# Two of the four down sums of the first feed-forward half: from VectorE's adds in SBUF to ScalarE copies and accumulating DMAs into DRAM

## The chip, the cores and the metric

The kernel runs on one core of a Trainium2 chip. The metric is the device time of one execution in microseconds. In profiles the engines are PE (TensorE: matmuls, with PEld for the loading of their stationary operand), DVE (VectorE), ACT (ScalarE), POOL (GpSimd) and SP (SyncE, which only issues DMAs here). An engine works through its own instructions in the order of the program. ScalarE and GpSimd can also issue DMAs, and such an issue stands in the engine's order like any other instruction: if it has to wait, everything behind it on that engine waits too.

## The reference

The kernel computes one transformer block on 2048 tokens of width 576: an attention with a compressive memory, then a SwiGLU feed-forward network. The change lies in the second. With h the normalised and modulated input, gb a gate and x the stream after the attention:

```python
def _B_ref(x, w_gate, w_up, w_down):      # w_gate, w_up: 576 x 4608, w_down: 4608 x 576
    g = _silu(x @ w_gate)
    u = x @ w_up
    return (g * u) @ w_down
...
h = _layernorm(x, axis=-1) * (1 + cb) + sb
x = x + gb * _B_ref(h, B_w_gate, B_w_up, B_w_down)
```

All inputs and outputs are fp32.

## The kernel before

The attention takes about the first third of the time. Its last step adds its result to the input and stores the stream x to DRAM (`xD`, four tensors of 512 tokens, each 128 partitions x 4 x 576). The feed-forward part then runs in two halves of 1024 tokens: t = 0 and t = 1. Each half is a loop over 18 pairs of 128-wide slices of the hidden dimension (p = 0 to 17), and each pair has 14 steps (k = 0 to 13).

*Gate and up products.* For a pair, gate (z = 0) and up (z = 1) are each computed by seven products of a Strassen-like scheme, one per step (`step`, `prod`, line 1202: seven matmuls of 512 columns). The products are gathered in three PSUM banks A, B and C. After the first product of a z, ScalarE copies bank A to a new bank B (line 1248, "B<-A"); the next product that adds to A, two steps later, has to wait for that copy. Two more copies (line 1231, "tb", "tc") play the same part later. `fin` (lines 1215 to 1226) joins banks and copies into the activations.

Every operand of a matmul is split into a rounded high part (a copy by ScalarE, lines 1166, 1191, 1266: `wh`, `dh`, `ah`) and a low rest (a subtraction by VectorE, lines 1167, 1192, 1267: `wl`, `dl`, `al`). The splits of weights are made five steps ahead of their product.

*Weights.* The gate and up weights of a pair come into two tiles `O` (z = 0 and 1). In the half t = 0 GpSimd makes the sums of weight blocks that the scheme needs (`sum_o`, line 1157), four per tile, in the steps 4 to 7 for z = 0 of the next pair and in the steps 10 and 11 for z = 1. These sums are stored to DRAM for the second half (`store_o`, line 1141, "oD<-O"), and ScalarE issues these stores: for z = 0 at step 11, for z = 1 at step 13, the last step of a pair. A tile O can be loaded again once VectorE has made the last `wl` from it. GpSimd also scales the down weights (`mul_d`, line 1180) and makes their sums (`sum_d`, line 1185), which ScalarE's queue stores at step 12 (line 1525, "wd").

*Down sums of the first half.* The down product of a pair is worked off in the steps of the next pair. `plain` handles one of its 8 chunks, in the steps 4 to 11: c runs over b (which 512 tokens), h (which 288 of the 576 output columns) and a half of the tokens. A chunk is twelve matmuls of 288 columns into two PSUM banks `pd` (two such buffers), and VectorE adds the result to an fp32 accumulator in SBUF (line 1327). There are four accumulators, `acc[2 + h + 2 * b]`; each is loaded beforehand with the matching part of `xD` (`load_res`, in steps that the table `RS` lists), so that it ends as the output. After the last pair it is stored to the output by a DMA that ScalarE issues (`store`, line 1295), three steps after its last chunk. The last pair of the first half is thus worked off in the first loop (p = 0) of the second half.

In the second half the down product is also done by a seven-product scheme (`down`, line 1306) with seven accumulators; `new_acc` makes three of them (1, 6, 7) when the pool `p6`, with the working tiles of `prep2` (the preparation of the second half's input), is closed.

The order of the work is written out by hand: the loops over p and k issue everything, and an engine gets its instructions in that order.

Of the kernel before, what the change touches and what calls it, by code (L numbers as in the profile page):

```python
# [7 lines left out]
F32 = mybir.dt.float32  # L8
# [3 lines left out]
ALU = mybir.AluOpType  # L12
# [3 lines left out]
P = 128  # L16
# [19 lines left out]
NSG = 7  # L36
CH = (1, 1, 1, 1, 2, 1, 0, 1, 1, 1, 1, 2, 1, 0)
CH0 = ((0, 0, 0, 0, 1, 1, 1, 1, 1, 1, 1, 1, 0, 0), (0, 0, 0, 1, 1, 1, 1, 1, 1, 1, 1, 0, 0, 0))
RS = {(0, 5): 2, (0, 6): 4, (0, 8): 3, (0, 10): 5, (1, 9): 2, (1, 11): 3, (1, 13): 4}
KS = (2, 3, 4, 5)  # L40
KA = ((5, 3), (6, 5), (7, 7), (3, 8))
ASRC = {5: (1, 1), 6: (0, 0), 7: (0, 1), 3: (1, 0)}
# [30 lines left out]
def block(ctx: ExitStack, tc: tile.TileContext, x, wqk, wv, wo, beta, wgu, wd, c, w_mod, out):  # L73
    nc = tc.nc
    def pool(stk, name, bufs=1, **kw):
        return stk.enter_context(tc.tile_pool(name=name, bufs=bufs, reuse_waits="tile", **kw))
# [9 lines left out]
    def run(g):  # L86
        for _ in g:
            pass
# [56 lines left out]
    xD = [dr.tile([P, 4, D], F32, tag=f"xD{s}", name=f"xD{s}") for s in range(NSEG)]  # L145
# [769 lines left out]
    NPR = NF // 2  # L915
# [362 lines left out]
    def new_acc(accp, ms):  # L1278
        for m in ms:
            acc[m] = accp.tile([P, 4, 288], F32, tag=f"acc{m}", name=f"acc{m}")  # L1280
# [3 lines left out]
    def load_res(t, m):  # L1284
        b, h = RES[m]
        nc.sync.dma_start(acc[m], xD[2 * t + b][:, :, 288 * h:288 * h + 288])
# [5 lines left out]
    def store(t, b, h, src, c=None):  # L1292
        r = 1024 * t + 512 * b
        i0, i1 = (0, 4) if c is None else (2 * c, 2 * c + 2)
        (nc.sync if t else nc.scalar).dma_start(out[r + 128 * i0:r + 128 * i1, 288 * h:288 * h + 288].rearrange("(i p) d -> p i d", p=P),
                          src[:, i0:i1])
# [16 lines left out]
    def plain(t, p, c):  # L1313
        b, h, c = c // 4, c // 2 % 2, c % 2
        pd = ps.tile([P, 2, L], F32, tag="dn", name="pd", bufs=2)
        for i in range(2):
            tk = slice(128 * (2 * c + i), 128 * (2 * c + i) + 128)
            k = 0
            for f in range(2):
                ah, al = AP[p % 2, (f, b)]  # L1320
                dh, dl = DP[p % 2, (f, h)]
                for a, w in ((ah, dh), (ah, dl), (al, dh)):
                    nc.tensor.matmul(pd[:, i, :288], lhsT=a[:, tk], rhs=w, start=(k == 0), stop=(k == 5))  # L1323
                    k += 1
        d = x11[1] if t and b and h else acc[2 + h + 2 * b]
        o = d[:, 2 * c:2 * c + 2]
        nc.vector.tensor_tensor(o, o, pd[:, :, :288], op=ALU.add)  # L1327
        if p == NPR - 1:
            if t:
                store(t, b, h, d, c)  # L1330
            elif c == 1:
                return lambda: store(t, b, h, d)

    def comb(j):
        d, b = ((2, 1), (0, 5), (6, 1), (5, 6), (3, 5), (7, 6), (4, 7), (0, 7))[j]
        d = acc[d] if d else x11[1]
        nc.vector.tensor_tensor(d, d, acc[b], op=ALU.add)

    def is_plain(t, p):
        return t == 0 or p >= NPR - 2  # L1340

    with tc.manual_schedule():
# [85 lines left out]
        p6 = ExitStack()  # L1428
# [12 lines left out]
        for t in range(2):  # L1441
            for p in range(NPR):
# [4 lines left out]
                if t == 0 and p == 1:  # L1447
                    p7.close()
                    x2p = pool(p6, "x2p")
                    g2 = prep2(x2p)  # L1450
                if t == 0 and p == NPR - 1:
                    run(g2)
                    p6.close()
                    accq = pool(p4, "acq")
                    new_acc(accq, (1, 6, 7))
# [3 lines left out]
                for k in range(14):  # L1459
# [68 lines left out]
                    if prev is not None and is_plain(*prev):  # L1528
                        if k in (0, 2):
                            ij = (1, 0) if k == 0 else (0, 1)  # L1530
                            prep_a(prev[1] % 2, ij, PA[ij])
                        if CH0[t][k]:
                            f = plain(*prev, chunk)
                            if f:
                                late[k + 3] = f
                            chunk += 1
                        due(k)
                    elif prev is not None:
                        for j in range(4):
                            if k == KS[j]:  # L1540
                                sum_a(j)
                        if k == 0:
                            prep_a(prev[1] % 2, 2, PA[1, 0])
                        for j, kk in KA:
                            if k == kk:
                                prep_a(prev[1] % 2, j, PA[ASRC[j]])
                        for _ in range(CH[k]):
                            down(*prev, chunk)
                            chunk += 1
                    if last and 1 <= k < 9:  # L1550
                        comb(k - 1)
                    if p == 0 and (t, k) in RS:
                        load_res(t, RS[t, k])
                    if is_plain(t, p):
# [20 lines left out]
        for c in range(8):  # L1575
            plain(*prev, c)
            if c == 0:
                flush()
# [52 lines left out]
```

## Time and profile before

| | |
|---|---|
| median of 3 runs | 1906.63 us |
| lowest, highest | 1906.19, 1909.42 us |
| span of the profiled execution, first to last instruction | 1906.7 us |
| TensorE busy | 1870.6 us (98%) |
| VectorE busy | 1507.7 us (79%) |
| ScalarE busy | 933.8 us (49%) |
| GpSimd busy | 579.1 us (30%) |

The profile gives the span of its execution and no other time of it. It shows one execution. A busy share is that of an engine's instructions; issues of DMAs are not counted as busy. A row of the groups names a line of the kernel, the engine, the operation, the tile written and the tiles read, the shapes and the count, then the busy time and the mean of one in ns, and after the second bar the idle time of the engine just before them with what ended it. Rows of the timeline begin with the start and the length in us and end, in brackets, with the idle time before and its releaser; ACTq and SPq are DMA issues of ScalarE and SyncE. A row of the chain of waits has start, length and what ran. A row of the waits says who waited for whom: in total, how often, and the longest.

### The profile page before, as it was taken

What the parts mean: (1) busy time and instruction counts of PE and PEld (TensorE: products, weight loads), DVE (VectorE), ACT (ScalarE), POOL (GpSimd) and SP (SyncE); (2) the same over time, 40 slices, a digit from 0 to 9 for tenths busy, and PEclk for the clock granted to TensorE, in tenths of its full rate; (3) what the DMA queues carried; (4) which work ended last, traced back from release to release, by engine and by line L of the source; (5) the groups of instructions that cost most, each with busy time, mean ns of one, the idle gap of its engine ahead of it and who ended that gap; (6) DMA issues with size and microseconds to landing.
All of it is one profiled execution on the core that took longest, in us unless ns stands there. A gap on an engine that the chain in (4) does not pass through costs nothing.

```text
span 1906.7 us, 30703 instructions
## 1 busy us (share of the span) xinstructions
PE 1870.6 (98%) x10927; PEld 1560.4 (82%) x10927; DVE 1507.7 (79%) x3277; ACT 933.8 (49%) x2060; POOL 579.1 (30%) x783
## 2 busy tenths in 40 slices
PE   7999999999999999999999999999999999999999
PEld 4878866676766788888888888888888888888888
DVE  6566358878886888888888888867888888888887
ACT  1222267768767543454454454444445454454542
POOL 5212236455556545445445435400000000000000
PEclk9999999999999999999999999999999999999999
DMA  6767555446654854554454554477333333333331
GB/s 196 253 216 251 200 191 155 131 137 172 186 159 134 301 204 148 170 190 142 170 188 139 186 162 129 152 258 237 102 124 102 98 103 101 123 102 104 104 106 61
DMA packets 179424, 304.31 MB, mean 160 GB/s; under 512 B 26152, under 2 KB 107688, under 8 KB 177352
## 3 DMA queue, kind: packets, MB, share of 16 engines
q1 hardware_dynamic: 150696, 245.29, 41.2%
q10 hardware_dynamic: 28576, 57.07, 8.4%
q8 instruction: 86, 1.41, 0.3%
q14 instruction: 66, 0.54, 0.1%
HBM read 187.98 MB, written 113.77 MB: 158 GB/s over the span
## 4 chain that ended last, share of the span: by engine, by line
PE 91%; DVE 3%; ACT 2%; DMA 2%; POOL 1%; issue 1%; SPq 0%; ACTq 0%; POOLq 0%; DVEq 0%
PE A L1202 23%; PE pd L1323 13%; PE C L1202 12%; PE pd L1306 9%; PE B L1202 6%; PE pp L99 5%; PE s L599 4%; PE av L619 4%; PE s L182 4%; PE pv L99 3%; PE pw L729 3%; PE pn L800 1%; ACT Pt L602 1%; PE px L640 1%; PE pm L448 1%
## 5 line engine op out<-in xcount | busy, mean ns | idle before, releaser
L1202 PE MATMUL A<-y,wh 128*128 128x512 f32 x1152 | 406.3, 393 | 3.1 <-ACT B L1248 2.5
L187 DVE CUSTOM_DVE_ANT_0 junk<-s,tri 128x256 bf16<-128x256 f32 (+3 forms) x512 | 228.5, 486 | 69.0 <-PE s L182 61.8
L1167 DVE TENSOR_TENSOR wl<-O,wh 128x256 fp32r<-128x256 f32 x504 | 262.1, 525 | 3.4 <-ACT wh L1166 2.9
L1202 PEld LDWEIGHTS A<-y,wh 128*128 128x128 f32 x1152 | 217.1, 188 | 47.0 <-ACT B L1248 3.2
L1202 PE MATMUL A<-y,wl 128*128 128x512 f32 x576 | 226.9, 394 | 0.0
L602 ACT ACTIVATE Pt<-s 128x512 f32<-128x512 f32 (+1 forms) x352 | 187.9, 559 | 70.9 <-PE s L599 66.6
L1157 POOL TENSOR_TENSOR O<-O 128x384 f32<-128x384 f32 x140 | 159.4, 1151 | 175.9 <-DMA O<-in_wgu_dram 73.8
L1311 DVE TENSOR_TENSOR acc<-acc,pd 128x576 f32<-128x576 f32 x216 | 162.3, 752 | 58.7 <-PE pd L1306 52.1
L1202 PE MATMUL C<-y,wh 128*128 128x512 f32 x576 | 203.3, 394 | 2.8 <-DMA y<-yD 2.4
L1166 ACT CAST wh<-O 128x256 fp32r<-128x256 f32 x504 | 196.7, 405 | 0.7 <-issue 0.7
L1323 PE MATMUL pd<-dh,al 128*128 128x288 f32 x640 | 189.0, 295 | 0.0
L1323 PE MATMUL pd<-dh,ah 128*128 128x288 f32 x640 | 188.9, 295 | 0.0
L1323 PE MATMUL pd<-dl,ah 128*128 128x288 f32 x640 | 188.8, 295 | 0.0
L1327 DVE TENSOR_TENSOR acc<-acc,pd 128x576 f32<-128x576 f32 x156 | 116.8, 749 | 87.9 <-PE pd L1323 87.6
L1266 ACT CAST ah<-sg 128x512 fp32r<-128x512 f32 x192 | 119.1, 620 | 86.5 <-DVE sg L1226 80.2
L599 PE MATMUL s<-qs,ks 110*128 110x512 f32 (+2 forms) x384 | 150.0, 407 | 3.7 <-ACT Pt L602 2.4
L182 PE MATMUL s<-ks,qs 108*128 108x256 f32 (+3 forms) x512 | 140.3, 326 | 3.2 <-DVE mx L187 3.1
L1267 DVE TENSOR_TENSOR al<-sg,ah 128x512 fp32r<-128x512 f32 x192 | 134.1, 699 | 8.6 <-ACT ah L1266 8.3
L1306 PE MATMUL pd<-dh,ah 128*128 128x288 f32 x448 | 133.0, 297 | 0.0
L1306 PE MATMUL pd<-dh,al 128*128 128x288 f32 x448 | 132.5, 296 | 0.0
L1306 PE MATMUL pd<-dl,ah 128*128 128x288 f32 x448 | 132.3, 295 | 0.0
L1202 PEld LDWEIGHTS C<-y,wh 128*128 128x128 f32 x576 | 108.5, 188 | 23.8 <-DMA y<-yD 2.8
(361 smaller groups left out, 4404.9 us busy)
## 6 DMA issues: line engine op xcount, KB each, us to landing
O<-in_wgu_dram SPq DMA_DIRECT2D x36, 768.0 KB
oD<-O ACTq DMA_DIRECT2D x36, 512.0 KB
O<-oD SPq DMA_DIRECT2D x36, 512.0 KB
ks<-kD SPq DMA_DIRECT2D x64, 216.0 KB
qs<-qD SPq DMA_DIRECT2D x64, 216.0 KB
O<-in_wgu_dram SPq DMA_DIRECT2D x36, 384.0 KB
rD<-wr ACTq DMA_DIRECT2D x36, 336.0 KB
wr<-rD SPq DMA_DIRECT2D x35, 336.0 KB
```

Source lines behind the costliest of these rows:

```text
L99: nc.tensor.matmul(ps, lhsT=a, rhs=b, start=(k == 0), stop=(k == 13))
L182: nc.tensor.matmul(bank[:, n * (h - h0):n * (h - h0) + n], lhsT=qst[b][0:108, h, 128 * i:128 * i + 128], rhs=kst[b][0:108, h // 2, 0:n], s ...
L187: nc.vector.tensor_tensor_reduce(junk[:, :n], bank[:, n * (h - h0):n * (h - h0) + n], tri[:, L - n:], 1.0, -3e38, op0=ALU.add, op1=ALU.max ...
L599: nc.tensor.matmul(bank[:, n * (g - h):n * (g - h + w)].rearrange("p (a b) -> p a b", a=w), lhsT=kst[u % NB][0:110, g // 2, 128 * j:128 * ...
L602: nc.scalar.activation(pt[:, h:h + per, :n], bank[:, :n * per].rearrange("p (a b) -> p a b", a=per), AF.Exp, scale=SCALE)
L1157: eng.tensor_tensor(o[:, d], o[:, a], o[:, b], op=op)
L1166: nc.scalar.copy(wh, o)
L1167: later.append(lambda: nc.vector.tensor_tensor(wl, o, f32(wh), op=ALU.subtract))
L1202: nc.tensor.matmul(bank, lhsT=a, rhs=b, start=(first and n == 0), stop=(n == 6), skip_group_check=not first)
L1306: nc.tensor.matmul(pd[:, i, :288], lhsT=a[:, tk], rhs=w, start=(k == 0), stop=(k == 2))
L1311: nc.vector.tensor_tensor(o, o, pd[:, :, :288], op=ALU.add)
L1323: nc.tensor.matmul(pd[:, i, :288], lhsT=a[:, tk], rhs=w, start=(k == 0), stop=(k == 5))
```

## The change

In the first half the two accumulators with h = 1 are no longer used. Their chunks are copied from PSUM by ScalarE into one of two staging tiles, and GpSimd issues a DMA that adds the tile to `xD` in DRAM. `xD` already holds the residual, so it is not loaded for these two (two entries of `RS` go), and the output of h = 1 is stored by a DMA from `xD` to the output. Chunks 2, 3, 6 and 7 of each pair are concerned: 4 x 18 = 72 adds of VectorE become 72 copies of ScalarE and 72 DMAs of GpSimd's queue. The staging tiles lie in the pool `p6`, which is therefore closed one loop and a bit later (in the second half, at p = 1), and so the three accumulators of the second half are made there.

```diff
-RS = {(0, 5): 2, (0, 6): 4, (0, 8): 3, (0, 10): 5, (1, 9): 2, (1, 11): 3, (1, 13): 4}
+RS = {(0, 5): 2, (0, 6): 4, (1, 9): 2, (1, 11): 3, (1, 13): 4}
...
                     k += 1
+        if t == 0 and h:
+            st = accs.tile([P, 2, 288], F32, tag="as", name="as")
+            nc.scalar.copy(st, pd[:, :, :288])
+            nc.gpsimd.dma_start(xD[b][:, 2 * c:2 * c + 2, 288:576], st, accum_op=ALU.add)
+            if p == NPR - 1 and c == 1:
+                return lambda: store(t, b, h, xD[b][:, :, 288:576])
+            return
         d = x11[1] if t and b and h else acc[2 + h + 2 * b]
...
                 if t == 0 and p == 1:
                     p7.close()
                     x2p = pool(p6, "x2p")
+                    accs = pool(p6, "accs", 2)
                     g2 = prep2(x2p)
                 if t == 0 and p == NPR - 1:
                     run(g2)
+                if t == 1 and p == 1:
                     p6.close()
                     accq = pool(p4, "acq")
                     new_acc(accq, (1, 6, 7))
```

## The prediction

> **What bounds the kernel now.** I read the page first, then busy time by stretch, then the waits of TensorE in the stage that changes.
>
> ```profile
> span 1906.7 us, 30703 instructions
> ...
> PE 1870.6 (98%) x10927; PEld 1560.4 (82%) x10927; DVE 1507.7 (79%) x3277; ACT 933.8 (49%) x2060; POOL 579.1 (30%) x783
> ```
>
> ```profile
> core 0: us, PE busy (x) PEld busy (x) DVE busy (x) ACT busy (x) POOL busy (x), PEclk, DMA share, GB/s
> 704.00:1276.00 572.00, 571.33 (x3152) 503.79 (x3151) 483.31 (x730) 271.09 (x630) 259.55 (x235) 1.00 0.51 167
> 1276.00:1312.00 36.00, 36.00 (x198) 31.67 (x197) 20.52 (x41) 14.73 (x36) 0.00 (x0) 1.00 0.96 310
> ```
>
> The 72 sums that move lie between 704 and 1312 us: 16 loops of 35.75 us (p = 1 to 16, less their first microseconds, and p = 17), then the first loop of the second half. TensorE is busy in 607.33 of these 608 us, at a granted clock of 1.00. Its waits there are these (first its matmuls', then its weight loads'):
>
> ```profile
> PE pt L1102 <- DMA xb<-xh: 0.7, 2, 0.5
> ```
> ```profile
> PEld A L1202 <- ACT B L1248: 0.3, 1, 0.3
> PEld pd L1323 <- DVE acc L1327: 0.2, 1, 0.2
> ```
>
> So TensorE, whose instructions stay in the same order, bounds the stage, and the adds that the change takes off VectorE held it up by 0.2 us in all. A relieved VectorE can return at most 608 - 607.33 = 0.67 us.
>
> **The change part by part.** Durations in these stretches, and one ScalarE copy from the first stage for the slope:
>
> ```profile
> L1327 DVE TENSOR_TENSOR acc<-acc,pd 128x576 f32<-128x576 f32 x136 | 101.9, 749 | 80.2 <-PE pd L1323 80.0
> L1231 ACT COPY tc<-A 128x512 f32<-128x512 f32 x34 | 19.9, 586 | 57.7 <-PE A L1202 57.3
> L496 ACT COPY vs<-pv 128x288 f32<-128x288 f32 x32 | 12.8, 400 | 51.4 <-PE pv L99 51.4
> L1157 POOL TENSOR_TENSOR O<-O 128x384 f32<-128x384 f32 x120 | 135.6, 1143 | 161.6 <-DMA O<-in_wgu_dram 63.3 <-DVE sg L1217 24.1 <-issue 19.9
> ```
>
> *VectorE* loses 72 x 0.749 = 53.9 us. It already sat idle before these adds until TensorE had finished; worth 0 to -0.67 us, taken as 0.
>
> *ScalarE* gains 72 copies of 128x576. From (586 - 400)/224 = 0.83 ns per element, one costs 586 + 64 x 0.83 = 639 ns: 46 us, 2.6 us per loop, where ScalarE was busy 271.09/16 = 16.9 of 35.75 us. What counts is where they stand in its order. Loop 816 to 848 us as an example:
>
> ```profile
> 824.56 0.60 ACT L1215 ACTIVATE sg<-A 128x512 f32<-128x512 f32 x1 [1.78 <-PE A L1202]
> 825.06 0.42 ACT L1191 CAST dh<-dr__10636 128x288 fp32r<-128x288 f32 x1
> 827.82 0.57 ACT L1248 COPY B<-A 128x512 f32<-128x512 f32 x1 [1.73 <-PE A L1202]
> 840.60 0.59 ACT L1231 COPY tc<-A 128x512 f32<-128x512 f32 x1 [3.31 <-PE A L1202]
> 843.88 0.52 ACTq L1141 DMA_DIRECT2D oD<-O  x1
> 846.09 0.62 ACT L1266 CAST ah<-sg 128x512 fp32r<-128x512 f32 x1 [3.69 <-DVE sg L1226]
> 846.62 0.40 ACT L1166 CAST wh<-O 128x256 fp32r<-128x256 f32 x1
> 847.02 0.57 ACT L1248 COPY B<-A 128x512 f32<-128x512 f32 x1
> ```
> ```profile
> 838.98 0.75 DVE L1327 TENSOR_TENSOR acc<-acc,pd 128x576 f32<-128x576 f32 x1 [0.48 <-PE pd L1323]
> ```
>
> A step with a down sum takes some 3.2 us (824.56 to 827.82), its product 1.62 of them (a row below), so TensorE finishes the four h = 1 sums at about 826.2, 829.4, 838.98 (the row) and 842.2 us. The first copy ends at 826.85; behind it stand dh (825.06 before) and two weight casts, done at 827.9, just as B's input is ready (827.82). The third ends at 839.6, ahead of tc (840.60); the second and fourth fall into idle time of ScalarE. dh arrives some 2 us later, but its product is used in the next loop. The bank is freed at 826.85, where VectorE's add had run from 827.49. Cost 0, covered by ScalarE's idle time.
>
> *The staging tiles.* There are two, so the third copy waits until the first one's transfer has landed. GpSimd in the same loop, then the load that its second group of sums needs:
>
> ```profile
> 827.21 1.02 POOL L1185 TENSOR_TENSOR dr__10636<-dr__10636 128x288 f32<-128x288 f32 x1
> 828.20 1.25 POOL L1157 TENSOR_TENSOR O<-O 128x384 f32<-128x384 f32 x1
> 831.26 1.76 POOL L1185 TENSOR_TENSOR dr__10636<-dr__10636 128x288 f32<-128x288 f32 x2
> 839.07 4.78 POOL L1157 TENSOR_TENSOR O<-O 128x384 f32<-128x384 f32 x4 [6.05 <-DVE sg L1222]
> ```
> ```profile
> 833.37 0.35 SPq L1135 DMA_DIRECT2D O<-in_wgu_dram  x1
> ```
> ```profile
> O<-in_wgu_dram SPq DMA_DIRECT2D x36, 768.0 KB
> ```
>
> The first transfer is issued after the operation that ends at 828.2. Even with 1.2 us of issue and the 5.7 us that the 768 KB load took (833.37 to 839.07; the transfer has 128 x 576 x 4 B = 288 KB, but reads its target too) it lands by 835.1, 3.9 us ahead of the third copy. Cost 0.
>
> *GpSimd's queue.* It gets 72 accumulating DMAs. No row shows one. The issue itself, X, I bound below by 0.52 us (ScalarE's DMA issue above) and above by 5.7 us (GpSimd held until such a load has landed). I take X = 1.2 us, the row of its own mean operation (1.143 us), since it is work of that engine. The Trainium skill, "DMA: Bandwidth & Descriptors", Specifications, gives about 1 us to the first byte on the gpsimd path; by that the sum is the same. Four issues a loop add 4.8 us to 16.2 busy; the engine keeps 14 us idle.
>
> What queues behind them matters. The first two stand among the sums that end at 833.02; with 2X these end at 835.4, ahead of 839.07. The third stands inside the second group (after two of its four sums, by the order of the program), so that this group ends at 843.85 + 1.2. ScalarE's store oD waits for that group (843.85, issued 843.88), and behind the store stand ah, wh and the copy B that TensorE needs two steps later. That this chain reaches TensorE is shown once, in the first loop, where GpSimd was late:
>
> ```profile
> 665.01 2.86 POOL L1157 TENSOR_TENSOR O<-O 128x384 f32<-128x384 f32 x2
> ```
> ```profile
> 667.91 0.52 ACTq L1141
> ...
> 670.07 0.49 ACT B L1248
> ...
> 670.61 1.43 PE A L1202 x5
> ```
> ```profile
> 670.61 0.50 PE L1202 MATMUL A<-y,wh 128*128 128x512 f32 x1 [2.47 <-ACT B L1248]
> ```
>
> The margin: B's input is ready at 847.0, TensorE works 1.62 us on another bank (row below), and from the store to the end of B pass 0.52 + 0.52 + 0.40 + 0.57 = about 2.1 us. So the store may be issued until 847.0 + 1.6 - 2.1 = 846.5: 2.7 us later than now. Another loop:
>
> ```profile
> 904.20 1.62 PE A L1202 x7
> ```
> ```profile
> 1057.33 0.52 ACTq L1141 DMA_DIRECT2D oD<-O  x1
> ...
> 1061.91 0.57 ACT L1248 COPY B<-A 128x512 f32<-128x512 f32 x1
> ```
>
> Here it is 1061.9 - 0.5 - 1057.3 = 4.1 us. Of the 16 loops three have 2.7 to 2.9, the others about 4.2. X = 1.2 is covered in all. If not, a loop pays X + max(0, 2X - 6.05) less its margin: free up to X = 2.7, beyond about 3.4 in every loop.
>
> The Trainium skill speaks against the change here: "SBUF — State Buffer", A bandwidth-pool intuition that's wrong, has such a DMA take 3.1 instead of 0.62 us beside a VectorE copy, since descriptors cannot be written. With X = 3.1 three loops pay 0.4 us, 1908.9 us with the last step below. The page ties it to two-port VectorE modes; the groups shown above are tensor_tensor, so I do not count on it.
>
> *The turn of the halves.* GpSimd is idle there, but the DMA engines are full:
>
> ```profile
> 1279.00:1287.00 8.00, 8.00 (x46) 7.14 (x45) 3.94 (x8) 3.50 (x8) 0.00 (x0) 1.00 1.03 328
> ```
> ```profile
> 1299.52 0.43 ACT L1191 CAST dh<-dr__15756 128x288 fp32r<-128x288 f32 x1 [3.96 <-DMA dr__15756<-wd]
> ...
> 1301.62 0.57 ACT L1231 COPY tb<-A 128x512 f32<-128x512 f32 x1
> ...
> 1307.80 0.59 ACT L1231 COPY tc<-A 128x512 f32<-128x512 f32 x1 [4.33 <-PE A L1202]
> ```
>
> Four accumulations fall between 1263 and 1297. Each moves 0.295 MB in up to three passes (read, read target, write), 2.7 us at 328 GB/s: together 0 to 10.7 us on the load that ScalarE awaits until 1299.52. The copy tb behind it ends at 1302.2; TensorE needs it when the step that ends at 1307.80 starts, 1306.2: 4.0 us of margin. Some accumulations come behind or beside the load, so I take half, 5 us: +1.0 us (0 to +6.7). Two of the result stores now go from DRAM to DRAM, three steps (over 9 us) behind their last accumulation, against about 7 for issue and landing: 0. The two residual loads that fall away at the start held nobody: 0.
>
> **Sum.** 1906.7 + 0 + 0 + 0 + 1.0 = 1907.7 us. The profiled execution gives no time but its span, 1906.7, which is 0.07 above the median of the runs (1906.63), so nothing is added around it. Those runs spread over 1906.19 to 1909.42, 0.17%; 0.2% (3.8 us) is about what a measurement can tell from no change.
>
> **The rivals.**
> 1. GpSimd's issue is long (slower): the third issue delays the second group of sums, this the store, this B. It decides from X = 2.7 us. At X = 4, 4 + 1.95 - 4.2 = 1.75 us in 13 loops and 3.2 in three: +32 us, 1940. For it: no row prices X, and the chain cost 2.47 us once. Against it: margins of 2.7 to 4.2 us. Chance 0.14 (the skill's starved descriptors would be this rival).
> 2. Transfers arrive later (slower): accumulations beside the load of 833.37 delay it. At 4 us, 1.2 + 4 - 4.2 = 1.0 in 13 loops and 2.5 in three make +20 us, 1928; the turn of the halves may add up to 6.7. For it: the share there is 0.96. Against it: 0.51 before. Chance 0.14.
> 3. ScalarE waits for a staging tile, or one copy stands ahead of a cast that TensorE needs: half a microsecond in 16 loops is 8 us, 1915. Against it: 3.9 us of margin. Chance 0.09.
> 4. Faster: VectorE's relief shows. At most 0.67 us are there (1906.0); more than 3.8 us would need time outside the changed stage. Chance 0.03.
> 5. The change does not do what it says: TensorE's order is unchanged and the adds leave VectorE's queue, so none is left for it.
>
> **How the numbers follow.** My forecast, no measurable change, has 0.60; its own range is 1906 to 1910. Rivals 1 to 3 make 0.37 slower, rival 4 0.03 faster. For eight in ten the range goes from 1905.5 to 1930: it takes in rivals 2 and 3 and leaves out most of rival 1.
>
> **What would show it.** Right: TensorE busy over 607 of 608 us in the changed stretches, an issue on GpSimd near 1.2 us, oD later by about that, B still on time, ScalarE near 19.5 us a loop, VectorE near 27.2. Wrong: TensorE waiting for B once per loop (rivals 1, 2; the longer of GpSimd's issue and the O load's landing tells which), ScalarE's copy waiting for a transfer (rival 3), or a wait at the turn of the halves well over 1 us.

## The result, and the profile after

The changed kernel took 1943.81 us (median of 4 runs, 1940.06 to 1946.76) against 1906.74 for the kernel before on the same chip: a ratio of 1.0186, with a 95% interval from 1.0173 to 1.0198. It is 37 us slower; the prediction had 1907.7. The profiled execution is the shortest of the four (1940.06 us) and its span is 31.7 us longer than that of before. The page of the kernel after, span and busy time:

```profile
span 1938.4 us, 30910 instructions
...
PE 1883.0 (97%) x10927; PEld 1563.6 (81%) x10927; DVE 1535.1 (79%) x3205; ACT 975.8 (50%) x2132; POOL 651.3 (34%) x855
```

VectorE (DVE) has 72 instructions fewer than before (3205 against 3277) and is busy 27 us longer (1535.1 against 1507.7). That is the first thing to explain. The two stretches of the change, in the columns of the prediction (us, then busy us and instructions of PE, PEld, DVE, ACT, POOL, then clock, DMA share and GB/s):

```profile
704.00:1276.00 572.00, 564.32 (x3086) 491.41 (x3086) 504.85 (x652) 303.63 (x682) 319.66 (x297) 1.00 0.72 192
1276.00:1312.00 36.00, 32.32 (x159) 27.59 (x158) 13.98 (x27) 11.46 (x25) 3.67 (x3) 0.91 1.06 345
```

TensorE, busy 571.33 of 572 us before, now stands 7.7 us in the first stretch; VectorE does 652 instructions in 504.85 us where it did 730 in 483.31. GpSimd's DMA issues, unlike those of the other engines, are counted as its instructions and as busy (855 are the 783 of before and 72 issues).

Where the 31.7 us lie is read best from one instruction that both kernels issue in the same order, ScalarE's copy of A to B. Its start in the kernel before, at three places (the start of the loops, their last, and two copies into the second half):

```profile
654.61 0.57 ACT L1248 COPY B<-A 128x512 f32<-128x512 f32 x1 [0.41 <-PE A L1202]
...
1241.99 0.57 ACT L1248 COPY B<-A 128x512 f32<-128x512 f32 x1
...
1312.59 0.57 ACT L1248 COPY B<-A 128x512 f32<-128x512 f32 x1 [0.33 <-PE A L1202]
```

and the same three copies after the change:

```profile
649.15 0.57 ACT L1248 COPY B<-A 128x512 f32<-128x512 f32 x1 [0.42 <-PE A L1202]
...
1252.76 0.58 ACT L1248 COPY B<-A 128x512 f32<-128x512 f32 x1
...
1344.55 0.58 ACT L1248 COPY B<-A 128x512 f32<-128x512 f32 x1
```

The differences are -5.5, +10.8 and +32.0 us; from the next copy on it stays at 31.2. So, before rounding, the loops of the first half lose 16.2 us, about 1 us each, and the turn of the halves 20.5. Below, "loops" and "turn" are these two numbers, from these copies, for every kernel. The offset at the start differs from kernel to kernel (-5.5 to +5.0 us) and is no part of either. Of the 16.2 us, 4.1 are lost by the fourth copy (705.14 us in the kernel before), with three issues so far; what cost them was not settled. The other 12.2 us fit the 66 matmuls that TensorE is short of in the first stretch (3086 against 3152, some 12 us at the pace of before); the 7.7 us of standing are less, as the ends of matmuls in the profile are modelled.

**In the loops** TensorE's weight loads wait for VectorE or for what stands behind it (waits of the kernel after, 704 to 1278 us; us in total, times, longest):

```profile
PEld A L1202 <- ACT B L1248: 6.7, 11, 0.7
PEld C L1202 <- DVE cu L1225: 6.0, 6, 1.9
PEld A L1202 <- ACT tb L1231: 3.8, 5, 1.0
```

Its matmuls wait for the same three: 3.5 us for `cu`, 2.1 for B and 1.8 for `tb`, 7.4 of the 7.7. One such place, VectorE after the change:

```profile
1062.75 1.16 DVE L1192 TENSOR_TENSOR dl<-dr__13047,dh 128x288 fp32r<-128x288 f32 x1
1063.84 3.23 DVE L1062 TENSOR_TENSOR st<-ha,st 128x256 fp32r<-128x256 f32 x1
1066.99 0.41 DVE L1167 TENSOR_TENSOR wl<-O,wh 128x256 fp32r<-128x256 f32 x1
1067.32 0.68 DVE L1267 TENSOR_TENSOR al<-sg,ah 128x512 fp32r<-128x512 f32 x1
1067.92 0.68 DVE L1225 TENSOR_TENSOR cu<-C,tc 128x512 f32<-128x512 f32 x1
1068.64 0.69 DVE L1226 TENSOR_TENSOR sg<-cu,sg 128x512 f32<-128x512 f32 x1
```

and GpSimd beside it:

```profile
1060.96 2.64 POOL L1157 TENSOR_TENSOR O<-O 128x384 f32<-128x384 f32 x2 [1.92 <-DVE wr L1152]
1063.54 1.22 POOL L1328 DMA_DIRECT2D xD<-as  x1
1064.32 2.45 POOL L1157 TENSOR_TENSOR O<-O 128x384 f32<-128x384 f32 x2
```

A subtraction of 128x256 that takes 0.41 us alone (as `wl` does right behind it) takes 3.23 us: it starts during GpSimd's issue of 1063.54 and ends at 1067.07, 0.30 us after the second of the sums that follow the issue (1064.32 + 2.45 = 1066.77). VectorE runs on without a gap, so `cu` ends at 1068.6, and TensorE's product at 1068.66 has stood 0.35 us waiting for it. Two microseconds on, `ah` waits for `sg`, B stands behind `ah`, and TensorE waits for B. At all 11 places where TensorE waited for B, `ah` had waited 2.9 to 5.2 us for `sg`.

Taken one by one, 39 VectorE instructions between 704 and 1276 us took 2 us or more; before, none did (the longest was 1.93). (The expectations below speak of 37, and of 27 for e11: they go by rows of the timeline that hold one instruction, and some of these stand in rows of two.) All 39 end 0.29 to 0.56 us after the end of an unbroken run of GpSimd's instructions, each begun before the last had ended, with an issue in it. The sums behind the issue are needed: of the 43 issues in this stretch with two or more sums right behind them 37 have such an instruction, of the 18 with one sum or none only 2. An issue by itself holds nothing: 9 of VectorE's subtractions began during an issue with nothing of GpSimd's within 0.3 us behind it, and all took 0.41 or 0.42 us. Those found long read SBUF alone. The adds with an operand in PSUM kept their time, in the groups of the kernel after from 704 to 1312 us:

```profile
L1334 DVE TENSOR_TENSOR acc<-acc,pd 128x576 f32<-128x576 f32 x66 | 49.4, 751 | 49.9 <-PE pd L1323 49.6
```

(749 ns before). The Trainium skill, "SBUF — State Buffer", Who interferes with whom, says that a VectorE instruction with two SBUF inputs contends with a GpSimd instruction that reads SBUF, and that the second to issue waits until the first is done. By that the subtraction would wait for one of GpSimd's sums, by estimate about 1.2 us. The kernel before agrees. Beside the four sums that run one behind another from 839.07 us, with no issue among them, VectorE gets in between:

```profile
840.39 1.38 DVE L1152 TENSOR_TENSOR wr<-O,wr 32x512 fp32r<-32x512 f32 x1
841.81 1.17 DVE L1192 TENSOR_TENSOR dl<-dr__10636,dh 128x288 fp32r<-128x288 f32 x1
```

These end 0.54 us after the second sum and 0.32 us after the third. The kernel after agrees that they contend, and differs in the length: behind an issue the subtraction waits for both sums, 2.8 us more than alone.

**At the turn** GpSimd computes nothing, and the waits are others. ScalarE after the change:

```profile
1288.81 0.64 ACT L1327 COPY as<-pd 128x576 f32<-128x576 f32 x1 [6.98 <-DMA xD<-as]
...
1313.45 0.64 ACT L1327 COPY as<-pd 128x576 f32<-128x576 f32 x1 [3.84 <-DMA xD<-as]
...
1320.25 0.64 ACT L1327 COPY as<-pd 128x576 f32<-128x576 f32 x1 [1.05 <-PE pd L1323]
1329.35 0.63 ACTq L1295 DMA_DIRECT2D out_dram<-xD  x1
1330.02 0.43 ACT L1191 CAST dh<-dr__15886 128x288 fp32r<-128x288 f32 x1 [9.13 <-DMA xD<-as]
...
1342.75 0.59 ACTq L1295 DMA_DIRECT2D out_dram<-xD  x1
1343.38 0.43 ACT L1191 CAST dh<-dr__15886 128x288 fp32r<-128x288 f32 x1 [9.18 <-issue]
```

and GpSimd's issues there, each long after the one before:

```profile
1301.64 1.23 POOL L1328 DMA_DIRECT2D xD<-as  x1 [11.40 <-issue]
1313.66 1.21 POOL L1328 DMA_DIRECT2D xD<-as  x1 [10.80 <-issue]
1320.01 1.22 POOL L1328 DMA_DIRECT2D xD<-as  x1 [5.13 <-ACT tb L1231]
1329.64 1.21 POOL L1328 DMA_DIRECT2D xD<-as  x1 [8.41 <-issue]
1337.46 1.22 POOL L1328 DMA_DIRECT2D xD<-as  x1 [6.61 <-issue]
```

The two stores of the h = 1 results stand in ScalarE's queue and wait there for the last accumulation into their half. Those issued at 1320.01 and 1337.46 release them at 1329.35 and 1342.75, and ScalarE stands 9.1 and 9.2 us. The second accumulation of the first half b had been ready when its copy ended (1313.45 + 0.64 = 1314.1): from there to landing it took 15.2 us. Each of the seven accumulations issued from 1276 us on starts 0.3 us after the one before it has landed. The DMA engines are full (a share of 1.06 in the second row above), and the accumulations issued from 1276 us on took 9.3 us in the median to land, those before 5.8.

### The profile page after: what moved, and what is told of

The parts are those of the page before. It is cut to its first block, busy times and chain, and to the rows that moved or that the text cites. A ratio compares the mean times of both kernels' runs of the same rounds, so it can differ in the third digit from the quotient of the medians.

```text
span 1938.4 us, 30910 instructions
## 1 busy us (share of the span) xinstructions
PE 1883.0 (97%) x10927; PEld 1563.6 (81%) x10927; DVE 1535.1 (79%) x3205; ACT 975.8 (50%) x2132; POOL 651.3 (34%) x855
## 4 chain that ended last, share of the span: by engine, by line
PE 76%; DVE 10%; issue 6%; ACT 2%; POOL 2%; DMA 2%; SPq 0%; ACTq 0%; DVEq 0%; POOLq 0%
PE A L1202 18%; PE pd L1306 9%; PE C L1202 9%; PE pd L1323 8%; PE pp L99 5%; PE B L1202 4%; PE s L599 4%; PE av L619 4%; PE s L182 4%; PE pv L99 3%; DVE wl L1167 3%; PE pw L729 3%; DVE dl L1192 1%; DVE wr L1152 1%; DVE st L1062 1%
## 5 line engine op out<-in xcount | busy, mean ns | idle before, releaser
L1202 PE MATMUL A<-y,wh 128*128 128x512 f32 x1152 | 412.4, 399 | 13.8 <-ACT tc L1231 5.9
L1167 DVE TENSOR_TENSOR wl<-O,wh 128x256 fp32r<-128x256 f32 x504 | 279.0, 558 | 4.5 <-ACT wh L1166 4.0
L1311 DVE TENSOR_TENSOR acc<-acc,pd 128x576 f32<-128x576 f32 x216 | 162.3, 751 | 58.9 <-PE pd L1306 52.3
L1157 POOL TENSOR_TENSOR O<-O 128x384 f32<-128x384 f32 x140 | 169.6, 1269 | 102.1 <-DVE sg L1217 32.7
L1267 DVE TENSOR_TENSOR al<-sg,ah 128x512 fp32r<-128x512 f32 x192 | 137.8, 717 | 15.8 <-ACT ah L1266 15.4
L1328 POOL DMA_DIRECT2D xD<-as x72 | 87.6, 1216 | 162.4 <-issue 91.8
```

The source lines that it names most:

```text
L1157: eng.tensor_tensor(o[:, d], o[:, a], o[:, b], op=op)
L1167: later.append(lambda: nc.vector.tensor_tensor(wl, o, f32(wh), op=ALU.subtract))
L1202: nc.tensor.matmul(bank, lhsT=a, rhs=b, start=(first and n == 0), stop=(n == 6), skip_group_check=not first)
```

## The experiments

Each row is a kernel below: issue on GpSimd (mean ns), packets of GpSimd's queue, VectorE's busy us between 704 and 1276, its instructions of 2 us or more there (one by one), loops and turn in us, and the median time. The loops of after, e4 and e12 hold the same instructions and come to 16.2, 18.2 and 15.8, so less than some 2.5 us between two kernels says little. The kernel before, run beside each of them, had medians of 1906.7 to 1910.0 us; the ratios below are to that one.

```
kernel                      issue  packets  VectorE  >=2us  loops   turn   median
before                          -        -   483.31      0      0      0  1906.7
after                        1216    19584   504.85     39   16.2   20.5  1943.8
e1 copies only                  -        -   461.77      0   -1.7    0.4  1907.1
e2 plain, SyncE                 -        -   461.69      3   -0.4    4.7  1911.2
e3 plain, GpSimd              737     5760   486.56     34    1.6    1.7  1913.3
e4 stores by GpSimd          1217    19872   510.57     40   18.2   10.4  1935.0
e5 four staging places       1216    19584   512.26     40   20.9   18.5  1947.1
e6 issue in idle time        1216    19584   417.73     13  120.8   24.7  2052.5
e7 whole rows                 949    10112   487.67     31    8.2    8.5  1923.9
e8 = e6 + e4                 1217    19872   412.66     13  125.9    7.8  2041.2
e9 few packets, idle          933     5472   463.11      7    4.5   12.1  1922.7
e10 few packets, at once      887     5472   456.55     13    1.6    8.6  1922.7
e11 before + small DMAs       531     2304   512.06     32   12.5   -0.4  1922.2
e12 no accumulation at turn  1216    17408   508.34     37   15.8    0.3  1928.0
e13 = e11, issue in idle      503     2304   479.88      2    0.1   -0.5  1908.0
```

### e1: the copies alone

```diff
             nc.scalar.copy(st, pd[:, :, :288])
-            nc.gpsimd.dma_start(xD[b][:, 2 * c:2 * c + 2, 288:576], st, accum_op=ALU.add)
```

> The 72 ScalarE copies into the staging tiles stay, the 72 accumulating transfers are left out, so the h = 1 half of the first half's output holds the residual alone. Theory A (GpSimd's issue holds VectorE: 37 VectorE instructions between 704 and 1276 us took 2 us or more in the changed kernel, none in the kernel before) and theory B (the traffic of the transfers makes loads and stores late) both expect the time of before or up to 5 us less (the first copy of A to B in the loops stood 5.5 us earlier in the changed kernel): 1901 to 1907 us, no VectorE instruction of 2 us. Theory C (the copies stand in ScalarE's way) expects most of the loss of the loops to stay: 1918 us or more.

1907.07 us, a ratio to before of 0.9997 (0.9985 to 1.0009). The first stretch of this kernel:

```profile
704.00:1276.00 572.00, 572.00 (x3157) 505.03 (x3156) 461.77 (x667) 309.99 (x695) 263.36 (x235) 1.00 0.51 169
```

TensorE does not stand at all, VectorE is 21.5 us lighter, and the time is that of before. So the 72 copies on ScalarE cost nothing, VectorE's relief is worth nothing, and all of the loss comes with the transfers. Theory C is out.

### e2 and e3: plain transfers, by SyncE and by GpSimd

```diff
+    sD = [dr.tile([P, 4, 576], F32, tag=f"sD{b}", name=f"sD{b}") for b in range(2)]
...
-            nc.gpsimd.dma_start(xD[b][:, 2 * c:2 * c + 2, 288:576], st, accum_op=ALU.add)
+            nc.sync.dma_start(sD[b][:, 2 * c:2 * c + 2, 288:576], st)      # e2
+            nc.gpsimd.dma_start(sD[b][:, 2 * c:2 * c + 2, 288:576], st)    # e3
```

> The same copies, and each staging tile is written by a plain transfer of SyncE's queue into a spare DRAM tile of the same shape; nothing is added, so the h = 1 half of the first half's output holds the residual alone. The bytes move, but GpSimd issues nothing. Theory A: no VectorE instruction of 2 us, the loops cost nothing, 1901 to 1912 us (something may be lost where SyncE's loads queue behind a transfer that waits for its copy). Theory B: the loops lose about 1 us each as before, 1918 to 1930 us.

> The same copies, and each staging tile is written by GpSimd's queue into a spare DRAM tile of the same shape, without adding; the h = 1 half of the first half's output holds the residual alone. Theory A: what holds VectorE is the issue, not the adding, so 30 to 40 VectorE instructions of 2 us or more stay between 704 and 1276 us, the 16 loops lose about 16 us, and only the turn of the halves (about 21 us) gets shorter: 1915 to 1935 us. If the adding is what costs: the held instructions go or the gaps between issues fall well below 4.7 us, 1901 to 1910 us.

e2: 1911.23 us (1.002, 1.001 to 1.003), the loops at -0.4: the bytes by themselves cost them nothing. Of its 4.7 us at the turn, 2.5 are one wait of TensorE for a load of y. e3: 1913.27 us (1.0031, 1.0018 to 1.0043). It came out between the two expectations. The held instructions stayed, 34 of them, but the loops lost only 1.6 us:

```profile
704.00:1276.00 572.00, 571.24 (x3148) 502.84 (x3147) 486.56 (x666) 308.54 (x693) 288.90 (x299) 1.00 0.61 200
```

Against e1, VectorE is busy 486.56 - 461.77 = 24.8 us longer with the same work. That uses up what the change had taken off it (it stands 3 us above before), and no more; in the kernel after it is 21.5 us above before. So the holding has to be weighed against the relief, and theory A in its first form, any issue costs a loop 1 us, was too simple. The total alone does not decide either: e7 below has VectorE at 487.67 us, as e3, and its loops lose 8.2. The queues of the two kernels show what adding changes, first after, then e3 (packets, MB, share of 16 engines; then KB each and median us to landing):

```profile
q0 software_dynamic: 19584, 21.24, 8.1%
...
xD<-as POOLq DMA_DIRECT2D x72, 288.0 KB, 5.9
```

```profile
q0 software_dynamic: 5760, 21.24, 3.2%
...
sD<-as POOLq DMA_DIRECT2D x72, 288.0 KB, 3.6
```

The same bytes go in 272 packets for each transfer instead of 80, the issue takes 1216 ns instead of 737, and two issues never follow within less than 4.68 us (2.65 in e3). The traces show why: in the kernel after, none of the 71 later accumulations starts before the one ahead of it has landed, and 45 start within 0.45 us of that landing; in e3, 11 start sooner. In the trace the program does not ask for this: the waits ahead of an accumulation are for ScalarE's copy and for the accumulation four before it, which had landed 24 us or more earlier.

### e4 and e5: the stores off ScalarE, and four staging places

The edit of e4, then that of e5:

```diff
-        (nc.sync if t else nc.scalar).dma_start(out[r + 128 * i0:r + 128 * i1, 288 * h:288 * h + 288].rearrange("(i p) d -> p i d", p=P),
+        (nc.sync if t else nc.gpsimd if h else nc.scalar).dma_start(out[r + 128 * i0:r + 128 * i1, 288 * h:288 * h + 288].rearrange("(i p) d -> p i d", p=P),
```

```diff
-            st = accs.tile([P, 2, 288], F32, tag="as", name="as")
+            st = acc[3 + 2 * b][:, 2 * c:2 * c + 2]
...
-                    accs = pool(p6, "accs", 2)
```

> The changed kernel in full, with the two stores of the h = 1 results (DRAM to DRAM) issued by GpSimd's queue in place of ScalarE's. If the 9.1 and 9.2 us that ScalarE stood behind them at 1320 to 1343 us are what TensorE lost last at the turn of the halves (B came 12.7 us later there), the time falls by 10 to 14 us: 1930 to 1934 us. If the staging tiles or SyncE's late loads are behind it, it stays within 3 us of 1943.8.

> The changed kernel in full, but the four copies of a loop go to four places (the residual tiles acc3 and acc5, which stand unused in the first half), so a copy waits for a transfer of the loop before and no longer for the one two before it. If the staging tiles cost the time (rival 3 of the prediction: ScalarE waited 10.8 us for landings at the turn of the halves, and 28.6 us for no named reason in the loops), the turn gets some 6 to 12 us shorter and the loops may too: 1925 to 1938 us. If they don't: within 3 us of 1943.8, as the next waits (the two stores on ScalarE) take their place.

e4: 1935.03 us (1.0147, 1.0126 to 1.0168). The turn falls from 20.5 to 10.4 us, as expected of the stores; the loops came out 2.0 longer. e5: 1947.07 us (1.0207, 1.019 to 1.0225), 3 us more than the changed kernel. The waits of ScalarE's copies for landings are gone, but the turn is still 18.5 us, as the two stores then wait as long. The staging tiles cost at most 2 us.

### e6 and e8: the issues behind GpSimd's sums

```diff
+            st = acc[3 + 2 * b][:, 2 * c:2 * c + 2]
             nc.scalar.copy(st, pd[:, :, :288])
+            if p < NPR - 1:
+                wait.append((xD[b][:, 2 * c:2 * c + 2, 288:576], st))
+                return
...
+                    if wait and k in (0, 2, 12, 13):
+                        d, s = wait.pop(0)
+                        nc.gpsimd.dma_start(d, s, accum_op=ALU.add)
```

> As the kernel with four staging places, and the four issues of a loop (all pairs but the last) stand at steps 12 and 13 and at steps 0 and 2 of the next loop, where GpSimd has no sums behind them. Theory A, refined (a VectorE instruction with both operands in SBUF is held from GpSimd's issue until the sums behind it end): at most 10 VectorE instructions of 2 us or more between 704 and 1276 us instead of 37, B's drift over the 16 loops falls from 16 us to below 4 us, and what is left is the turn of the halves: 1915 to 1932 us. If each accumulation costs by its traffic or by its issue alone, wherever it stands: the drift stays at 10 us or more, 1930 us or more.

> The kernel with four staging places and the issues in GpSimd's idle time, and the two stores of the h = 1 results issued by GpSimd's queue in place of ScalarE's: all three causes treated, the computation whole. If the three are all there is: the loops lose below 4 us and the turn about 5 to 9 us, 1909 to 1919 us. It does not get below 1903 us, since the copies alone gave 1907.1 (a ratio of 0.9997 to before): VectorE's relief is worth nothing. If a cause is missing: 1925 us or more.

2052.47 us (1.0775, 1.0747 to 1.0803) and 2041.22 (1.0706, 1.0687 to 1.0725). Both are over 100 us above the ranges that were expected of a repair; by the letter they fall under "1930 us or more" and "1925 us or more", which had no such loss in mind. e6 has 13 held instructions where at most 10 were expected. GpSimd in e6:

```profile
1014.23 1.23 POOL L1563 DMA_DIRECT2D xD<-acc  x1 [6.03 <-issue]
1019.59 1.21 POOL L1563 DMA_DIRECT2D xD<-acc  x1 [4.13 <-issue]
1024.97 1.21 POOL L1563 DMA_DIRECT2D xD<-acc  x1 [4.17 <-issue]
...
1026.43 1.91 POOL L1180 TENSOR_TENSOR dr__12220<-dr__12220,gbB 128x576 f32<-128x576 f32 x1
```

and ScalarE and VectorE there, in the order of their starts:

```profile
1028.38 0.43 ACT L1191 CAST dh<-dr__12220 128x288 fp32r<-128x288 f32 x1 [8.44 <-POOL dr__12220 L1180]
```

```profile
1028.84 6.60 DVE L1192 TENSOR_TENSOR dl<-dr__12220,dh 128x288 fp32r<-128x288 f32 x1 [3.77 <-ACT dh L1191]
```

All copies had long been made, yet each issue starts 5.4 us after the last: GpSimd stands at an accumulation until the one before has landed, and its sums stand behind. With the last two issues ahead of the scaling of the down weights (L1180), ScalarE waits 8.44 us for that, PSUM banks are not freed, and TensorE waits (its matmuls into `pd` for ScalarE's copies 45.4 us in 11 waits between 704 and 1276 us). Then the sums that have piled up, in an unbroken run until 1035.1, hold one VectorE instruction for 6.60 us. The 13 held instructions of e6 took 6.5 to 8.6 us, and each ends 0.29 to 0.33 us after such a run, of 8 to 11 sums behind an issue. So the study's own repair met two things that the changed kernel shows less plainly: GpSimd stands at an accumulation until the one before has landed, and GpSimd can keep VectorE out as long as its run behind an issue lasts. In e8 the stores by GpSimd brought the turn to 7.8 us, again.

### e7, e9 and e10: fewer packets

```diff
-            nc.gpsimd.dma_start(xD[b][:, 2 * c:2 * c + 2, 288:576], st, accum_op=ALU.add)
+            nc.gpsimd.dma_start(aD[b][c], st, accum_op=ALU.add)    # e7: aD[b] is [2, P, 2, 288]
...
```

```diff
+    aD = [dr.tile([P, 4, 288], F32, tag=f"aD{b}", name=f"aD{b}") for b in range(2)]
+    def add(b):
+        nc.gpsimd.dma_start(aD[b], acc[3 + 2 * b], accum_op=ALU.add)
...
+            nc.scalar.copy(acc[3 + 2 * b][:, 2 * c:2 * c + 2], pd[:, :, :288])
...
+                    if wait and k in (12, 13):     # e9; in e10 add(b) stands right behind the second copy
+                        add(wait.pop(0))
```

> The changed kernel with the accumulations into a DRAM tile of its own, laid out so that each partition's 2 x 288 values are one run of 2304 B instead of two rows of 1152 B; the first pair's sums are written plainly, and the residual is left out of the h = 1 half of the first half's output. The bytes and the adding stay. If the number of packets sets the price (plain: 80 packets, 734 ns of issue, 3.6 us to landing; adding: 272 packets, 1213 ns, 5.9 us), it has some 144 packets and comes to 734 + 479 x 64/192 = about 890 ns and 4.4 us, and the loops lose about a third of their 16 us: 1924 to 1934 us. If the adding itself sets it: 1.2 us, 5.9 us, 1938 to 1947 us.

> The whole computation. The sums of h = 1 are added in a DRAM tile of their own (it starts as a copy of the residual), laid out with one run of 4608 B per partition; one accumulation for each half b instead of two, 36 in all, about 144 packets each; they stand at steps 12 and 13, behind GpSimd's sums, and the stores of the results are issued by GpSimd's queue. If the causes are the packets (GpSimd stands still until the descriptors before are worked off), the sums behind an issue (VectorE held), and at the turn of the halves ScalarE behind the stores: at most 8 VectorE instructions of 2 us, loops losing below 4 us, turn below 6 us: 1905 to 1916 us. If accumulation costs by its bytes: 1925 us or more, since the bytes are the same.

> As the kernel with one accumulation per half b and runs of 4608 B, but each is issued right behind the second copy (step 7, among GpSimd's sums, and step 11) in place of steps 12 and 13. If VectorE is held only where sums follow the issue: some 16 held VectorE instructions (that of step 7 in each loop), the loops lose 3 to 8 us more than with steps 12 and 13: 1910 to 1922 us. If the place doesn't matter: within 2 us of that kernel.

e7: 1923.87 us (1.0083, 1.0062 to 1.0103). Adding the same bytes in 144 packets takes off half of both losses (8.2 and 8.5 us left): 949 ns of issue (890 expected), but 6.2 us to landing (4.4 expected), so the landing does not go by the packets. What changed is the order: 36 of the 71 later transfers now start before the one ahead of them has landed, 2.29 us behind it at the least, and the time that GpSimd stands at these issues for no reason that the profile names falls from 35.7 us between 704 and 1276 us to 0.6. Whether the packets do this or the tile of its own, e7 does not part. e9: 1922.70 us (1.0076, 1.0061 to 1.0091). e10: 1922.66 (1.007, 1.0053 to 1.0086). With 36 issues the held instructions fall to 7 and 13, VectorE is as light as in e1, and the loops come to 4.5 (below 4 expected) and 1.6 us. The place of the issue made no difference that shows, against the 3 to 8 us expected for e10: 13 instructions were held there, near the 16 expected, and they cost the loops nothing that can be seen beside a VectorE without its adds. The turn was expected below 6 us and is 12.1 and 8.6, although no store of h = 1 stands on ScalarE: TensorE waits there for the loads of y and for VectorE, in e9 (1242 to 1340 us):

```profile
PE pd L1311 <- DVE acc L1316: 3.8, 2, 3.2
PE A L1202 <- DMA y<-yD: 2.1, 2, 1.3
PE B L1202 <- DMA y<-yD: 2.1, 2, 1.1
PE C L1202 <- DMA y<-yD: 1.3, 1, 1.3
```

### e12: no accumulation at the turn

```diff
+            if p < NPR - 2:
                 nc.gpsimd.dma_start(xD[b][:, 2 * c:2 * c + 2, 288:576], st, accum_op=ALU.add)
```

> The changed kernel without the last eight of its 72 accumulations (those of pairs 16 and 17, which fall from about 1258 us on); their copies stay, and the h = 1 half of the first half's output lacks these two pairs' sums. It splits the loss between loops and turn in the changed kernel itself. If the turn of the halves costs by the accumulations that land there in full DMA queues (21 us of B's drift, ScalarE's waits for landings and behind the two stores among them): 1920 to 1926 us, the drift from 1258 us on below 3 us, and ScalarE's waits for a landing gone. If the turn costs for another reason (the copies, the stores from DRAM to DRAM): it stays above 1935 us.

1927.95 us (1.0105, 1.0083 to 1.0127). The turn is 0.3 us, with copies, staging tiles and both stores from DRAM to DRAM in place; the loops keep their 15.8. The two losses are separate, and the whole of the second comes with the eight accumulations that land there.

### e11 and e13: small transfers beside the kernel before

```diff
         nc.vector.tensor_tensor(o, o, pd[:, :, :288], op=ALU.add)
+        if t == 0 and h:
+            nc.gpsimd.dma_start(sD[2 * b + c], o[0:16])    # e11; e13 issues them at steps 12 and 13
...
```

> The kernel before, whole, with VectorE's adds kept, and beside them 72 plain transfers of GpSimd's queue of 36 KB each (16 partitions of the sum just made, to a spare DRAM tile that nobody reads), issued where the changed kernel issues its accumulations. An eighth of the bytes, nothing added. Theory A (the issue takes VectorE's operands away until GpSimd's sums behind it end): 20 or more VectorE instructions of 2 us or more where before had none, and as VectorE keeps its adds (3 us a loop) it is late: 1915 to 1935 us. Theory B (the traffic): 1905 to 1910 us.

> The kernel before, whole, with the same 72 small plain transfers of GpSimd's queue, but issued at steps 12 and 13 (two each), behind GpSimd's sums and long after their data are there. If the loops lost their 12 us because VectorE is held from an issue until the sums behind it end, the held instructions nearly go (at most 6 instead of 27) and the drift over the loops falls below 3 us: 1905 to 1913 us. If the loss comes from the issues themselves wherever they stand: the drift stays at 10 us or more, 1918 us or more.

e11: 1922.22 us (1.006, 1.004 to 1.0079). An eighth of the bytes, nothing added, VectorE's adds where they were, and the loops lose 12.5 us; the turn loses nothing. In its first stretch VectorE is busy 28.8 us longer than before with the DMA share unchanged:

```profile
704.00:1276.00 572.00, 565.41 (x3086) 491.90 (x3085) 512.06 (x722) 266.74 (x623) 281.62 (x302) 1.00 0.51 164
```

VectorE and GpSimd in e11, one view each:

```profile
802.33 2.83 DVE L1192 TENSOR_TENSOR dl<-dr__10259,dh 128x288 fp32r<-128x288 f32 x1
```

```profile
802.03 0.53 POOL L1330 DMA_DIRECT2D sD<-acc  x1 [1.28 <-DVE acc L1328]
802.58 0.75 POOL L1110 TENSOR_TENSOR ha<-ha 128x256 f32<-128x256 f32 x1
803.28 1.57 POOL L1185 TENSOR_TENSOR dr__10259<-dr__10259 128x288 f32<-128x288 f32 x2
```

The same picture: begun during the issue and held to 0.31 us after the last sum (804.85). e13 moves these issues behind the sums and leaves all else: 1908.00 us, 1.0004 (0.9988 to 1.0021), 2 held instructions, loops 0.1, and

```profile
704.00:1276.00 572.00, 571.26 (x3149) 503.32 (x3148) 479.88 (x727) 270.27 (x627) 287.88 (x299) 1.00 0.54 172
```

TensorE is back at 571.26 of 572 us. What costs the loops here is thus neither the bytes nor the 72 issues as such, but issues with sums behind them. One thing this pair does not part: in e11 the issue also waits for VectorE's add, and the sums behind it with it. The held instructions account for the 28.8 us of VectorE; how much of the 12.5 us that waiting adds was not tried. Nor does it say why the changed kernel, with about as many held instructions as e3 (39 against 34), loses 16.2 us and not 1.6: its accumulations also make GpSimd stand, which e7 nearly ends, and e7 still loses 8.2. How the 16.2 us divide between the two was not settled.

## Why the prediction was wrong

*VectorE's relief is worth 0.* Right: e1 has it for itself, 0.9997.

*ScalarE's copies cost 0.* Right in price and size: 640 ns measured against 639 estimated, and e1 shows that they are hidden.

*GpSimd's issue, X.* The size was right, 1216 ns against 1.2 us. The step that failed is the sentence that costed the issue by its own time alone, 4.8 us a loop in 14 us of idle time, and passed over VectorE because "the groups shown above are tensor_tensor". The rule weighed there from the Trainium skill, "SBUF — State Buffer", A bandwidth-pool intuition that's wrong, that such a DMA is starved beside a copy of VectorE, is not what happened here: the issue kept its 1.2 us. The reverse did: VectorE's instructions on SBUF operands were kept waiting until the sums behind the issue had ended, and the engine that the change was to relieve got 21.5 us busier between 704 and 1276 us. The other half of the step also failed: issues do not only take 1.2 us each, GpSimd stands at the next one until the last has landed, so that they start 4.68 us apart at the least. The upper bound of X had this time (5.7 us, until a load has landed), but at the issue itself and not at the next. A dense stretch of VectorE, ending in `cu` and in the `sg` for which `ah` and B wait, had no slack for 2 to 3 us. This is where the loops lost their 16.2 us; that TensorE's waits there lead to VectorE is shown, the share of the holding and that of GpSimd's standing are not.

*Third issue, store oD, ah, B (rival 1).* At all 11 places where TensorE waited for B, ScalarE had waited for VectorE's `sg`, and the store had been issued 2.2 us or more before that wait ended; the rival's 1940 us is near the result, and its mechanism is not the one seen.

*Staging tiles.* In the loops the landing of 5.7 us was right (5.8 measured), and from 704 us to the turn no copy waited for one. At the turn the copies waited 7.0 and 3.8 us for landings, but four places took off only 2 us: nearly right as a sum, wrong as a picture.

*The turn of the halves.* The term for the delayed load (+1.0, bounds 0 to 6.7) and the term "two of the result stores ... over 9 us behind their last accumulation, against about 7 for issue and landing: 0" together gave 1.0 us; 20.5 were measured. The second failed by more: 15.2 us from the end of the copy to the landing, since the issue itself stood until the accumulation before had landed, and landings took 9.3 us in full queues. For the same reason the accumulations bunched: seven were issued from 1276 us on, one behind another, the last at 1337.46. Taking the stores off ScalarE took 10 us off the turn (e4). Some 8 to 12 us stay with the accumulations however they are issued (e4, e7 to e10), and go when they go (e12). Which share of these is the loads of y behind the accumulations' traffic was not settled.

*The range and the chances.* The slower rivals went up to 1940 us, each priced alone, and the range ended at 1930; here a loss in the loops and one at the turn came together. The 0.60 for no change rested on a price found right for one engine, and on the silence of the profile about two others.

## What to carry to other kernels

An issue on GpSimd's queue is not paid by its own 0.5 to 1.2 us: count GpSimd's run of instructions behind it against every VectorE instruction that reads only SBUF, and place issues where nothing follows them (12.5 us against 0.1 for the same 72 plain transfers). That holds as long as an issue does not stand until the one before has landed: for accumulations of 272 packets the same move cost 120 us (e6). An accumulating DMA wants few, long rows (loops and turn halved in e7), and no urgent work behind it in any queue, neither GpSimd's next instruction nor another engine's store that reads its target. Before work is moved off an engine, ask whether its time bounds anything at all: here e1 shows that the most the change could bring was nothing.

## What the runs showed of the hardware that was not expected

VectorE's instructions on SBUF operands took 2 to 3.9 us instead of 0.4 to 1.2 beside GpSimd, and all 39 of them ended 0.29 to 0.56 us after GpSimd's unbroken run that held an issue. Without issues it is rare but not unknown: none in the kernel before and in e1, three in e2, the longest of 4.15 us (`wl` at 1145.09) beside an unbroken run of GpSimd's sums; e13 has two behind no issue. So an issue is not needed for it, but 37 of 43 with two or more sums behind them brought it on; why, no run here tells. The issue alone does not: VectorE's subtractions that began during one with no sum behind took 0.41 to 0.46 us in every kernel that has such a case (22 of them in e6). An accumulating transfer of 288 KB went in 272 packets where a plain one of the same shape went in 80, with 1216 against 737 ns of issue and 5.9 against 3.6 us to landing. GpSimd did not start the next accumulation of 272 packets until the one ahead had landed, in any of 71 cases, which makes 4.68 us between issues at the least; with 144 packets 36 of 71 started sooner, 2.29 us apart at the least.
